# Attention followed by a softplus feed-forward network on one core: new places for attention's steps, the words of `at` and of the rests, and the accumulators' copies in the written queues of VectorE and ScalarE

## Chip, cores and metric

One core of a Trainium2 chip runs the whole kernel. The metric is the device time of one execution in microseconds (us); lower is better.

## What is computed

For each of 8 batches and 8 heads, 32 pack queries `p` attend over 576 keys and values, and then the 576 queries `q` attend over the 32 packed results, which serve as keys and as values. The heads, side by side, are the rows of `x` (4608 x 512), which goes through a feed-forward network with a softplus between its two products:

```python
p_packed = sm_attn(p, k, v)              # softmax(scale * p k^T) v
x = sm_attn(q, p_packed, p_packed)       # then heads side by side
h = x @ w_in                             # 512 -> 2048
g = np.maximum(h, 0.0) + np.log1p(np.exp(-np.abs(h)))
out = g @ w_out                          # 2048 -> 512
```

All is float32. The large products are made from float32r words: each factor is split into a high word and a low word (the rounding error of the high one), and three products of words are added.

## The kernel before

The main loop goes through **units** (b, f): 8 batches times 16 blocks of 128 columns of the hidden layer (L808). A unit has these parts.

- `gemm1` (L646): 12 matmuls of 288 columns into two PSUM banks of the pool `ps_h`, `ph` for columns 0 to 287 (c = 0) and 288 to 575 (c = 1). The moving data are `at_h` and `at_l`, the high and low words of the second attention's weights, which `weights` (L596) makes once per batch; the stationary data are `mh` and `ml`, the words of the pack results times `w_in` (`make_m`, L617, from a PSUM tile `psm`).
- `softplus` (L681): ScalarE takes `Abs`, `Exp` and `Ln` of each half (L691 to L693), VectorE adds the maximum (`e`, L699), which is the last read of a `ph` bank, and then `split` (L677) makes the words `gh` and `gl` of the result. GpSimd copies the last 64 rows to `rest` (L707).
- `gemm2_tile` (L713): two units later (`LAG`), 4 tiles t of 3 matmuls of 512 columns, which add into 4 accumulator banks `acc`. After the last f the four are copied to SBUF by `store` (L733) and sent out. The 64 left-over rows of two batches are added together in `rests` (L748) after every second batch: 48 matmuls into `acc_m`, from words `gh_m`, `gl_m`, which are made 256 columns at a time into two places.

Batches 2 to 7 get their attention from `attention_in_slots` (L495): `at(f, t, step)` puts a step into unit f of the batch before, after tile t of `gemm2_tile`; t = `END` (4) is behind all four. Names of steps: `move` transposes one 128x288 block of k or q on VectorE (`T_k`, `T_q`, L276); `score1` and `score2` are score matmuls into tiles `ps`; with `pair` (L506) they take the two `ps_h` banks. `score1`'s result is copied out by ScalarE, `score2`'s is transposed out by VectorE (L379). `max1` is a maximum over 576 columns (L319) and a scaling (L321); `exp2` and `div2` are the second softmax (L387, L388; L396 to L403).

From unit 16 on (L815) VectorE and ScalarE run their instructions in the order in which the program writes them, as TensorE does throughout. In a unit of batch 1 or later, `softplus` writes ScalarE's six functions at the start, `e` of half 0 behind the steps of t = 0, `e` of half 1 behind those of t = 2, and the split behind those of t = 3. The eight banks of PSUM are 4 for `acc`, 2 for `ps_h`, 2 for `psm` and the rest.

Of the kernel before, what the change touches and what calls it, by code (L numbers as in the profile page):

```python
# [26 lines left out]
def pack_attention_then_softplus_ffn(  # L27
# [10 lines left out]
    nc = tc.nc  # L38
# [3 lines left out]
    P = 128  # L42
# [452 lines left out]
    def attention_in_slots(b):  # L495
# [55 lines left out]

        END = NT
        early = b == BY_BLOCK
        for hh in range(HG):
            if early:
                at(hh // 2, hh % 2 * 2 + 1, move, "k", 0, hh)
                at(2, hh, move, "k", 1, hh)
            else:
                at(hh // 2 - 3, hh % 2 * (1 + (hh < 2)) + (hh < 2), move, "k", 0, hh)
                at(hh // 2 * 2, hh % 2 * (1 + (hh < 2)) + (hh < 2), move, "k", 1, hh)  # L560
            at(3 + hh // 2, 1 + hh % 2 * 2, move, "q", 0, hh)
            at(9 + hh // 2, hh % 2 * (1 + (hh < 2)) + (hh < 2), move, "q", 1, hh)
        if early:
            steps[(b - 1) * NF + 2, 0].insert(0, (score1, (0, False)))
            n = 2
        else:
            at(-2, END, score1, 0)
            n = 0
        at(-2 if not early else 2, END, load, "q", b, 0)
        at(n, 1 if early else 0, max1, 0)  # L570
        at(n, 2, exp1, 0)
        n = 3 if early else 2
        at(n, 0, sum1, 0)
        at(n, 0, turn1, 0, 0)
        at(n, 2, turn1, 0, 1)
        at(2, END, score1, 1)
        at(2, END, load, "q", b, 1)
        at(4, 0, max1, 1)
        at(4, 0, exp1, 1)
        at(5, 0, sum1, 1)  # L580
# [7 lines left out]
        for g in range(G):  # L588
            f = 6 + 4 * g
            at(f, END, score2, g)  # L590
            at(f, END, load, "v", b + 1, g)
            for c in range(2):
                at(f + 2, 2 * c, exp2, g, c)
                at(f + 3 + c, 2 * c, div2, g, c)

    def weights(b):  # L596

        at_h = work.tile([P, G, S], F32R, tag="at_h", name=f"at_h_{b}", bufs=1)
        at_l = work.tile([P, G, S], F32R, tag="at_l", name=f"at_l_{b}", bufs=1)
# [12 lines left out]

    def m_cols(b):
# [32 lines left out]
    def gemm1(b, f, res):  # L646

        n = m_cols(b)
        halves = res["m"][f * P // n]
        at_h, at_l = res["at"]  # L650
        phs = []
        for c in range(2):
            ph = ps_h.tile([P, 512], F32, tag="h", name=f"ph_{b}_{f}_{c}")
            phs.append(ph[:, :C])
            todo = [(g, j) for g in range(G) for j in range(3)]
            if f == 0 and b >= BY_BLOCK:
                todo.sort(key=lambda x: x[1] == 1)
            for i, (g, j) in enumerate(todo):
                mh, ml = halves[g * n // MC]
                o = g * n % MC + f * P % n  # L660
                cs = slice(c * C, (c + 1) * C)
                x, y = ((mh, at_h), (mh, at_l), (ml, at_h))[j]
                nc.tensor.matmul(  # L663
                    ph[:, :C], x[:, o:o + P], y[:, g, cs],
                    start=(i == 0), stop=(i == 3 * G - 1),
                )
                if (b, f, i) == (0, 0, 0) and c == 0:
                    busy(30, "at_l", (ps_acc, "acc"))
        return phs

    def halves(nm):
# [58 lines left out]
    def out_tile(nm):  # L730
        return cv.tile([P, 2, DM], F32, tag="x", name=f"o_{nm}", bufs=2)

    def store(o, acc, pieces, final=False):  # L733
        if final:
            n = DM // 2
            nc.vector.tensor_copy(o[:, :n], acc[:, :n])
            nc.scalar.copy(o[:, n:], acc[:, n:])
        else:
            nc.vector.tensor_copy(o, acc)  # L739
        for i, (row, b, col, n) in enumerate(pieces):  # L740
            queue = nc.scalar if final and i else nc.sync
            while n:
                to = rows_of(b, col)
                m = min(n, to.shape[0])
                queue.dma_start(to[:m], o[row:row + m, :])
                row, col, n = row + m, col + m, n - m

    def rests(b):  # L748


        fs = sorted(range(NF), key=lambda x: rest_at(b, x))
        gh, gl = halves(f"{b}_m")
        n = NT // 2
        for i in range(0, NF, n):
            o = rest_at(b, fs[i])
            c = i % NT * P
            cs = slice(c, c + n * P)
            split(gh[:, cs], gl[:, cs], rest[:, o:o + n, :].rearrange("x f j -> x (f j)"))
            if i == 0:
                yield  # L760
                am = ps_acc.tile([P, DM], F32, tag="acc", name=f"acc_{b}_m")
            for t in range(n):
                gemm2_tile(
                    am, gh, gl, fs[i + t], slice(c + t * P, c + (t + 1) * P),
                    i + t == 0, i + t == NF - 1,
                )
        pieces = [(0, b - 1, NT * P, REST), (REST, b, NT * P, REST)]
        store(out_tile(f"{b}_m")[:, 0], am, pieces, b == B - 1)
        yield


# [27 lines left out]
            next(conv)  # L799
            due -= 1  # L800
    make_m(0, 0, res[0])
    weights(0)
# [10 lines left out]
    for u in range(len(units) + LAG):  # L813
        if u == NF:
            ctx.enter_context(tc.manual_schedule(engines=ordered))  # L815
        if u < len(units):
# [24 lines left out]
        if last:  # L841
            both = rests(b2)
            next(both)
        for t in range(NT):
            if u >= LAG:
                gemm2_tile(
# [2 lines left out]
            if u < len(units):  # L849
# [56 lines left out]
```

## Time and profile before

| | us |
|---|---|
| median of 3 runs | 787.74 (786.58 to 788.06) |
| the profiled execution, its own time | 786.9 |
| its span | 785.1 |
| TensorE matmul busy | 745.4 (95% of the span) |
| VectorE busy | 552.9 (70%) |
| ScalarE busy | 464.7 (59%) |
| GpSimd busy | 91.6 (12%) |

The profiled execution's own time stands 1.8 us over its span and 0.8 us under the median. Busy time of TensorE is modelled from pipelined matmuls that overlap: a 288-column matmul is listed with 0.29 us, but the next starts 0.13 us later, so starts are to be compared, not durations. VectorE's and ScalarE's rows overlap a little as well.

### The profile page before, as it was taken

To read this page: it belongs to the slowest core of one execution; us is meant where nothing else is said; L and a number is where in the kernel's file an instruction comes from. 1 tells how busy PE (TensorE), PEld (TensorE's weight loads), DVE (VectorE), ACT (ScalarE), POOL (GpSimd) and SP (SyncE) were. 2 spreads that over 40 slices of the span, in tenths; PEclk is the share of its full clock that TensorE was granted. 3 is DMA by queue.
4 is the path that set the end of the run, shared out by engine and by line. 5 is a ranking of instruction groups with operands and counts; after the bars stand their busy time and mean duration, and the time that the engine had idled before them with its cause. 6 is when DMAs were issued, how large, how long until landed. Compare 5 with 4: busy or idle time off the path is not lost.

```text
span 785.1 us, 14466 instructions
## 1 busy us (share of the span) xinstructions
PE 745.4 (95%) x5436; PEld 595.5 (76%) x5436; DVE 552.9 (70%) x1264; ACT 464.7 (59%) x1086; POOL 91.6 (12%) x166
## 2 busy tenths in 40 slices
PE   6888998899999999999998999999999999999997
PEld 3766676678777887778886887788876787888886
DVE  2697899975877558776778568775778568775454
ACT  5668888565565455676555355666555355666650
POOL 1413443100000000000000000000000000000010
PEclk9878999999999999999999999999999999999999
DMA  9985756455222251125012251125113200010001
GB/s 213 239 186 150 180 157 153 81 108 99 40 33 57 44 91 31 31 78 97 10 26 70 58 92 30 28 72 92 18 31 71 58 2 1 1 54 1 1 1 68
DMA packets 163398, 55.98 MB, mean 71 GB/s; under 512 B 143872, under 2 KB 156672, under 8 KB 163328
## 3 DMA queue, kind: packets, MB, share of 16 engines
q1 hardware_dynamic: 162704, 54.80, 32.6%
q8 instruction: 42, 0.69, 0.4%
q10 hardware_dynamic: 624, 0.26, 0.1%
q14 instruction: 28, 0.23, 0.1%
HBM read 45.61 MB, written 9.44 MB: 70 GB/s over the span
## 4 chain that ended last, share of the span: by engine, by line
PE 66%; DVE 9%; ACT 4%; issue 1%; DVEq 0%; ACTq 0%
PE acc L715 33%; PE ph L663 21%; PE acc_m L715 5%; PE psm L625 3%; DVE e L699 2%; PE ps L294 1%; DVE at_l L607 1%; ACT e L692 1%; ACT e L693 1%; PE psa L339 1%; PE psp L353 1%; ACT e L691 1%; DVE gl L679 1%; DVE o L739 1%; DVE aT L403 1%
## 5 line engine op out<-in xcount | busy, mean ns | idle before, releaser
L691 ACT ACTIVATE e<-ph 128x288 f32<-128x288 f32 x256 | 103.0, 404 | 178.3 <-PE ph L663 161.1
L715 PE MATMUL acc<-wo_h,gh 128*128 128x512 f32 x512 | 204.2, 399 | 0.0
L715 PE MATMUL acc<-wo_l,gh 128*128 128x512 f32 x512 | 201.5, 394 | 0.0
L715 PE MATMUL acc<-wo_h,gl 128*128 128x512 f32 x512 | 201.3, 393 | 0.0
L699 DVE SCALAR_TENSOR_TENSOR e<-ph,e 128x288 f32<-128x288 f32 x256 | 114.5, 452 | 120.8 <-ACT e L693 120.8
L663 PE MATMUL ph<-at_h,mh 128*128 128x288 f32 x512 | 157.5, 308 | 8.9 <-DVE e L699 5.7
L663 PE MATMUL ph<-at_h,ml 128*128 128x288 f32 x512 | 151.3, 296 | 0.0
L663 PE MATMUL ph<-at_l,mh 128*128 128x288 f32 x512 | 149.9, 297 | 0.4 <-DVE at_l L607 0.2
L663 PEld LDWEIGHTS ph<-at_h,mh 128*128 128x128 f32 x512 | 96.8, 189 | 44.2 <-DVE a L379 11.4
L707 POOL COPY rest<-e 128x64 f32<-128x64 f32 x128 | 46.1, 361 | 590.6 <-DVE e L699 588.1
L692 ACT ACTIVATE e<-e 128x288 f32<-128x288 f32 (+1 forms) x240 | 110.6, 461 | 7.4
L693 ACT ACTIVATE e<-e 128x288 f32<-128x288 f32 (+1 forms) x240 | 110.6, 461 | 7.2
L715 PEld LDWEIGHTS acc<-wo_h,gl 128*128 128x128 f32 x512 | 96.5, 189 | 21.0
L715 PEld LDWEIGHTS acc<-wo_h,gh 128*128 128x128 f32 x512 | 96.5, 188 | 18.0 <-issue 2.3
L715 PEld LDWEIGHTS acc<-wo_l,gh 128*128 128x128 f32 x512 | 96.6, 189 | 14.8
L663 PEld LDWEIGHTS ph<-at_l,mh 128*128 128x128 f32 x512 | 96.4, 190 | 3.7 <-DVE at_l L607 1.0
L663 PEld LDWEIGHTS ph<-at_h,ml 128*128 128x128 f32 x512 | 96.8, 189 | 0.0
L679 DVE TENSOR_TENSOR gl<-e,gh 128x512 fp32r<-128x512 f32 x128 | 88.4, 691 | 8.3
L640 ACT CAST mh<-psm 128x512 fp32r<-128x512 f32 (+1 forms) x72 | 35.6, 541 | 46.6 <-PE psm L625 45.8
L678 DVE CAST gh<-e 128x512 fp32r<-128x512 f32 x128 | 55.8, 436 | 4.9
L641 DVE TENSOR_TENSOR ml<-psm,mh 128x512 fp32r<-128x512 f32 (+1 forms) x72 | 42.0, 621 | 19.7 <-ACT mh L640 19.7
L625 PE MATMUL psm<-w_in_sb,pt 64*32 64x512 f32 (+1 forms) x576 | 45.7, 561 | 2.4 <-DVE a L379 1.2
(79 smaller groups left out, 764.6 us busy)
## 6 DMA issues: line engine op xcount, KB each, us to landing
v<-in_v SPq DMA_DIRECT2D x16, 576.0 KB, 5.7
x_i<-in_moe_w_in SPq DMA_DIRECT2D x32, 256.0 KB, 4.5
x_o<-in_moe_w_out SPq DMA_DIRECT2D x16, 512.0 KB, 3.5
k<-in_k SPq DMA_DIRECT2D x48, 144.0 KB, 3.4
q<-in_q SPq DMA_DIRECT2D x48, 144.0 KB, 3.2
out<-o SPq DMA_DIRECT2D x24, 256.0 KB, 2.1
k<-in_k SPq DMA_DIRECT2D x4, 576.0 KB, 10.7
q<-in_q SPq DMA_DIRECT2D x4, 576.0 KB, 8.8
```

The lines of the kernel that those rows point to most:

```text
L625: nc.tensor.matmul(ps[hh * J:(hh + 1) * J, :n], res["pt"][g][o:o + D, hh * J:(hh + 1) * J], w_in_sb[o:o + D, hh, c * n:(c + 1) * n], start ...
L640: nc.scalar.copy(mh[:, cols], ps[:, :n])
L641: nc.vector.tensor_tensor(ml[:, cols], ps[:, :n], mh[:, cols].bitcast(F32), op=ALU.subtract)
L663: nc.tensor.matmul(ph[:, :C], x[:, o:o + P], y[:, g, cs], start=(i == 0), stop=(i == 3 * G - 1),)
L678: nc.vector.tensor_copy(hi, x)
L679: nc.vector.tensor_tensor(lo, x, hi.bitcast(F32), op=ALU.subtract)
L691: nc.scalar.activation(es[c], hv[c], AF.Abs)
L692: nc.scalar.activation(e[:, x], e[:, x], AF.Exp, scale=-1.0)
L693: nc.scalar.activation(e[:, x], e[:, x], AF.Ln, bias=1.0)
L699: nc.vector.scalar_tensor_tensor(es[c], hv[c], 0.0, es[c], op0=ALU.max, op1=ALU.add)
L707: nc.gpsimd.tensor_copy(rest[:, rest_at(b, f), r:r + REST], e[:, NT * P:])
L715: nc.tensor.matmul(acc, x[:, cs], y[:, f, :], start=(first and i == 0), stop=(last and i == 2),)
```

## The change

Four things move; nothing is computed differently.

1. Attention's steps get other places in the table: all `move` steps; `exp2` and `div2` of both halves go ahead of a unit's first `e`; `max1` of group 0 goes from ahead of unit 0's first `e` to behind it (in the steady batches), and in the first attention in slots (b = 2, `early`) the score and softmax steps of group 0 move by about a unit. In units with f = 10 (`late_split`) the split of `e` is written behind the steps of `END`.
2. `weights` becomes a generator: ScalarE casts `at_h` of group 0 only, VectorE casts group 1 (2 casts of 128x288 per batch), and `at_l` is made in two parts, on either side of unit 15's second `e`. In unit 0 of a batch, `gemm1` now runs all 8 products with `at_h` of both halves first and the 4 with `at_l` last, with the halves alternating.
3. `rests` makes two parts of its words before its first matmul, and each further part two groups of matmuls ahead.
4. The copies of accumulators 2 and 3 go from VectorE to ScalarE. The next pack of `p` is loaded in unit 1 and transposed in unit 6 (of batch 2), not 3 and 10.

```diff
+            moves = ((-4, 1), (-3, 1), (-2, 1), (-2, 3)), ((0, 1), (0, 2), (2, 0), (2, 1))
+        turns = ((2, END), (2, END), (3, 1), (4, 1)), ((8, 1), (9, 1), (10, 1), (10, 3))
...
-        at(n, 1 if early else 0, max1, 0)
-        at(n, 2, exp1, 0)
+        at(n, 1, max1, 0)
+        at(n, 1, exp1, 0)
...
-                at(f + 2, 2 * c, exp2, g, c)
-                at(f + 3 + c, 2 * c, div2, g, c)
+                at(f + 2, 0, exp2, g, c)
+                at(f + 3 + c, 0, div2, g, c)
...
+        for c in range(2):
+            high(nc.scalar.copy, 0, c)
+        yield
+        for c in range(2):
+            high(nc.vector.tensor_copy, 1, c)
+        for c in range(2):
+            low(0, c)
+        yield
+        for c in range(2):
+            low(1, c)
...
+        todo = [(c, g, j) for c in range(2) for g in range(G) for j in range(3)]
+        if f == 0 and b >= BY_BLOCK:
+            todo.sort(key=lambda x: (x[2] == 1, x[2] == 1 and x[1]))
...
+        for i in range(NT // n):
+            words(i)
+        yield
...
+            words(i + NT // n)
...
+    copies = nc.vector.tensor_copy, nc.scalar.copy
...
-                if f == 3:
+                if f == 1:
...
-                if f == 10:
+                if f == 6:
...
+        late_split = u < len(units) and b and f == 10
...
-            next(chain, None)
+            if not (late_split and t == NT - 1):
+                next(chain, None)
+            if t % 2 == 0:
+                next(words, None)
...
-                store(o[:, t % 2], acc[t], [(0, b2, t * P, P)])
+                store(o[:, t % 2], acc[t], [(0, b2, t * P, P)], copies[t // 2])
...
+            if late_split:
+                next(chain, None)
```

**Place 1: VectorE's queue in unit 10 of batch 4**, where attention of batch 5 makes its scores of group 1 (`ps_5_1_0`, `ps_5_1_1`). Before:

```order
L679 TENSOR_TENSOR gl_9_5767<-e_9_5733,gh_9_5766 128x512
L276 STREAM_TRANSPOSE T_q_1_2_5794<-q_1_5313 128x288
L699 SCALAR_TENSOR_TENSOR e_10_5784<-ph_10_0_5770,e_10_5784 128x288
L276 STREAM_TRANSPOSE T_q_1_3_5800<-q_1_5313 128x288
L396 TENSOR_REDUCE z_5_0_1_5805<-a_5_0_1_5609 128x9
L397 TENSOR_SCALAR z_5_0_1_5805<-z_5_0_1_5805 128x9
L398 RECIPROCAL z_5_0_1_5805<-z_5_0_1_5805 128x9
L399 TENSOR_TENSOR a_5_0_1_5609<-a_5_0_1_5609,z_5_0_1_5805 128x288
L403 STREAM_TRANSPOSE aT_0_1_5810<-a_5_0_1_5609 128x288
L699 SCALAR_TENSOR_TENSOR e_10_5784<-ph_10_1_5777,e_10_5784 128x288
L678 CAST gh_10_5817<-e_10_5784 128x512
```

The same place in the change:

```order
L403 STREAM_TRANSPOSE aT_0_1_5799<-a_5_0_1_5609 128x288
L716 SCALAR_TENSOR_TENSOR e_10_5784<-ph_10_0_5770,e_10_5784 128x288
L276 STREAM_TRANSPOSE T_q_1_2_5805<-q_1_5313 128x288
L716 SCALAR_TENSOR_TENSOR e_10_5784<-ph_10_1_5771,e_10_5784 128x288
L276 STREAM_TRANSPOSE T_q_1_3_5814<-q_1_5313 128x288
L379 STREAM_TRANSPOSE a_5_1_0_5822<-ps_5_1_0_5816 128x288
L379 STREAM_TRANSPOSE a_5_1_1_5828<-ps_5_1_1_5817 128x288
L695 CAST gh_10_5833<-e_10_5784 128x512
```

The five instructions of `div2` (from the reduction to `aT`) now stand ahead of both `e`, the fourth `T_q` stands behind the second `e`, and the two transposes that empty the score banks stand ahead of the split. Unit 14, with `T_k` and the next batch's `score1`, moves in the same way but keeps its split where it was.

**Place 2: VectorE's queue from unit 15 of batch 4 into unit 0 of batch 5** (`m_6_0` is `max1` of batch 6's attention). Before:

```order
L607 TENSOR_TENSOR at_l_6100<-aT_0_0_5748,at_h_6099 128x9x32
L607 TENSOR_TENSOR at_l_6100<-aT_0_1_5810,at_h_6099 128x9x32
L607 TENSOR_TENSOR at_l_6100<-aT_1_0_5972,at_h_6099 128x9x32
L607 TENSOR_TENSOR at_l_6100<-aT_1_1_6034,at_h_6099 128x9x32
L699 SCALAR_TENSOR_TENSOR e_15_6095<-ph_15_0_6081,e_15_6095 128x288
L699 SCALAR_TENSOR_TENSOR e_15_6095<-ph_15_1_6088,e_15_6095 128x288
```

The same place in the change:

```order
L716 SCALAR_TENSOR_TENSOR e_15_6095<-ph_15_0_6081,e_15_6095 128x288
L310 CAST at_h_6099<-aT_1_0_5974 128x9x32
L310 CAST at_h_6099<-aT_1_1_6023 128x9x32
L608 TENSOR_TENSOR at_l_6100<-aT_0_0_5750,at_h_6099 128x9x32
L608 TENSOR_TENSOR at_l_6100<-aT_0_1_5799,at_h_6099 128x9x32
L716 SCALAR_TENSOR_TENSOR e_15_6095<-ph_15_1_6082,e_15_6095 128x288
L608 TENSOR_TENSOR at_l_6100<-aT_1_0_5974,at_h_6099 128x9x32
L608 TENSOR_TENSOR at_l_6100<-aT_1_1_6023,at_h_6099 128x9x32
```

The first `e` no longer stands behind the four `at_l`, and two casts have come to VectorE.

**Place 3: VectorE's queue in unit 0 of batch 5.** Before:

```order
L319 TENSOR_REDUCE m_6_0_6155<-a_6_0_6045 128x1
L321 TENSOR_SCALAR nm_6_0_6157<-m_6_0_6155 128x1
L699 SCALAR_TENSOR_TENSOR e_0_6145<-ph_0_0_6131,e_0_6145 128x288
L276 STREAM_TRANSPOSE T_k_1_0_6163<-k_1_5522 128x288
L699 SCALAR_TENSOR_TENSOR e_0_6145<-ph_0_1_6138,e_0_6145 128x288
L276 STREAM_TRANSPOSE T_k_1_1_6174<-k_1_5522 128x288
```

The same place in the change:

```order
L716 SCALAR_TENSOR_TENSOR e_0_6145<-ph_0_0_6131,e_0_6145 128x288
L276 STREAM_TRANSPOSE T_k_1_0_6159<-k_1_5522 128x288
L319 TENSOR_REDUCE m_6_0_6161<-a_6_0_6045 128x1
L321 TENSOR_SCALAR nm_6_0_6163<-m_6_0_6161 128x1
L276 STREAM_TRANSPOSE T_k_1_1_6170<-k_1_5522 128x288
L716 SCALAR_TENSOR_TENSOR e_0_6145<-ph_0_1_6132,e_0_6145 128x288
```

Two transposes and the maximum now stand between the first and the second `e`.

## Rows read from the trace of the kernel before

In the timelines the columns are start, duration (both us), engine, line, operation, tiles out<-in, shapes, count, and in brackets the engine's idle time just before and what ended it.

**Rows 1.** The first part of the page, all engines: busy us (share of the span) and instructions.
```profile
PE 745.4 (95%) x5436; PEld 595.5 (76%) x5436; DVE 552.9 (70%) x1264; ACT 464.7 (59%) x1086; POOL 91.6 (12%) x166
```

**Rows 2.** The waits of TensorE from 150 us to the end: waiting line, releaser, total us, times, longest.
```profile
PE ps L294 <- DVE e L699: 5.8, 11, 1.5
PE acc_m L715 <- DVE gh_m L678: 3.8, 3, 1.3
PE ph L663 <- DVE e L699: 2.0, 6, 0.4
```

**Rows 3.** Timeline of TensorE at the end of unit 10 of batch 4: the two halves of `score2`, and the first `ph` matmul of unit 11 (`psm` in between).
```profile
486.83 0.69 PE L294 MATMUL ps<-T_q,pt 64*32 64x288 f32 x8
487.96 0.45 PE L294 MATMUL ps<-T_q,pt 64*32 64x288 f32 x4 [0.44 <-DVE e L699]
...
489.68 0.40 PE L663 MATMUL ph<-at_h,mh 128*128 128x288 f32 x1 [0.17 <-DVE a L379]
```

**Rows 4.** Timeline of VectorE in the same unit: first `e`, `T_q`, the start of `div2`, second `e`.
```profile
484.92 0.46 DVE L699 SCALAR_TENSOR_TENSOR e<-ph,e 128x288 f32<-128x288 f32 x1 [0.80 <-ACT e L693]
485.29 0.47 DVE L276 STREAM_TRANSPOSE T_q<-q 128x288 f32<-128x288 f32 x1
485.69 0.41 DVE L396 TENSOR_REDUCE z<-a 128x9 f32<-128x288 f32 x1
...
487.49 0.42 DVE L699 SCALAR_TENSOR_TENSOR e<-ph,e 128x288 f32<-128x288 f32 x1
```

**Rows 5.** Timeline of TensorE at the end of unit 2 of batch 5: the same kind of score block, and the `ph` behind it.
```profile
528.59 0.71 PE L294 MATMUL ps<-T_k,pT 64*32 64x288 f32 x16
...
530.09 0.40 PE L663 MATMUL ph<-at_h,mh 128*128 128x288 f32 x1
```

**Rows 6.** The same at the end of unit 14 of batch 4.
```profile
507.21 0.69 PE L294 MATMUL ps<-T_k,pT 64*32 64x288 f32 x8
...
509.81 0.40 PE L663 MATMUL ph<-at_h,mh 128*128 128x288 f32 x1
```

**Rows 7.** The same at the end of unit 10 of batch 2, the unit that begins with the transposes of the next pack.
```profile
308.08 0.88 PE L294 MATMUL ps<-T_q,pt 64*32 64x288 f32 x8
...
312.01 0.40 PE L663 MATMUL ph<-at_h,mh 128*128 128x288 f32 x1
```

**Rows 8.** The same at the end of unit 2 of batch 1, in the first attention in slots.
```profile
169.48 1.55 PE L294 MATMUL ps<-T_k,pT 64*32 64x288 f32 x11
...
172.06 0.40 PE L663 MATMUL ph<-at_h,mh 128*128 128x288 f32 x1
```

**Rows 9.** Timeline of ScalarE from unit 15 of batch 4 on: the casts of `at_h`, `Abs` and `Ln` of unit 15's second half, and `Abs` of the first half of unit 1.
```profile
512.23 1.42 ACT L310 CAST at_h<-aT 128x288 fp32r<-128x288 f32 x4
513.55 0.40 ACT L691 ACTIVATE e<-ph 128x288 f32<-128x288 f32 x1
...
514.46 0.44 ACT L693 ACTIVATE e<-e 128x288 f32<-128x288 f32 x1
...
520.21 0.41 ACT L691 ACTIVATE e<-ph 128x288 f32<-128x288 f32 x1 [0.96 <-PE ph L663]
```

**Rows 10.** Timeline of VectorE in the same stretch: `at_l`, the first `e` of unit 15; `max1`, the first `e` and a `T_k` of unit 0; the first `e` of unit 1.
```profile
512.67 1.57 DVE L607 TENSOR_TENSOR at_l<-aT,at_h 128x288 fp32r<-128x288 f32 x4 [1.27 <-ACT at_h L310]
514.15 0.45 DVE L699 SCALAR_TENSOR_TENSOR e<-ph,e 128x288 f32<-128x288 f32 x1
...
516.50 0.75 DVE L319 TENSOR_REDUCE m<-a 128x1 f32<-128x576 f32 x1
...
517.36 0.46 DVE L699 SCALAR_TENSOR_TENSOR e<-ph,e 128x288 f32<-128x288 f32 x1
517.73 0.47 DVE L276 STREAM_TRANSPOSE T_k<-k 128x288 f32<-128x288 f32 x1
...
521.67 0.46 DVE L699 SCALAR_TENSOR_TENSOR e<-ph,e 128x288 f32<-128x288 f32 x1 [1.21 <-ACT e L693]
```

**Rows 11.** Timeline of TensorE in the same stretch: the last `acc` matmul of unit 15, the first `ph` of unit 0, the first and the seventh `ph` of unit 1.
```profile
514.05 0.39 PE L715 MATMUL acc<-wo_h,gl 128*128 128x512 f32 x1
514.75 0.37 PE L663 MATMUL ph<-at_h,mh 128*128 128x288 f32 x1 [0.32 <-DVE e L699]
...
519.16 0.29 PE L663 MATMUL ph<-at_h,mh 128*128 128x288 f32 x1
...
519.95 0.29 PE L663 MATMUL ph<-at_h,mh 128*128 128x288 f32 x1
```

**Rows 12.** Timeline of TensorE in unit 1 of batch 4: the sixth and the seventh matmul of `acc_m`.
```profile
429.57 0.39 PE L715 MATMUL acc_m<-wo_h,gl_m 128*128 128x512 f32 x1
431.23 0.50 PE L715 MATMUL acc_m<-wo_h,gh_m 128*128 128x512 f32 x1 [1.27 <-DVE gh_m L678]
```

**Rows 13.** Timeline of VectorE there: the copy of accumulator 3, and the second part's high word.
```profile
430.29 0.68 DVE L739 COPY o<-acc 128x512 f32<-128x512 f32 x1
430.89 0.28 DVE L678 CAST gh_m<-rest 128x256 fp32r<-128x256 f32 x1
```

**Rows 14.** Timeline of VectorE in unit 8 of batch 4: first `e`, the maximum of `exp2`'s second half, second `e`.
```profile
476.26 0.46 DVE L699 SCALAR_TENSOR_TENSOR e<-ph,e 128x288 f32<-128x288 f32 x1 [0.67 <-ACT e L693]
476.64 0.44 DVE L387 TENSOR_REDUCE m<-a 128x9 f32<-128x288 f32 x1
...
477.49 0.45 DVE L699 SCALAR_TENSOR_TENSOR e<-ph,e 128x288 f32<-128x288 f32 x1
```

More of the change, by code (lines that the diff above doesn't have):

```diff
@@ L553, in attention_in_slots @@
         early = b == BY_BLOCK
[L554 to L562, printed above, removed]
-        if early:
-            steps[(b - 1) * NF + 2, 0].insert(0, (score1, (0, False)))
-            n = 2
+        if early:
+            moves = ((0, 1), (0, 2), (0, 3), (1, 0)), ((2, 0), (2, 0), (2, 1), (2, 3))
+        else:
+            moves = ((-4, 1), (-3, 1), (-2, 1), (-2, 3)), ((0, 1), (0, 2), (2, 0), (2, 1))
+        turns = ((2, END), (2, END), (3, 1), (4, 1)), ((8, 1), (9, 1), (10, 1), (10, 3))
+        for what, places in (("k", moves), ("q", turns)):
+            for g in range(G):
+                for hh, place in enumerate(places[g]):
+                    if (what, g, hh) == ("q", 0, 0):
+                        at(2, END, score1, 1)
+                        at(2, END, load, "q", b, 1)
+                    at(*place, move, what, g, hh)
+        if early:
+            at(1, 3, score1, 0, False)
+            at(1, 3, load, "q", b, 0)
+            n = 3
         else:
             at(-2, END, score1, 0)
+            at(-2, END, load, "q", b, 0)
             n = 0
-        at(-2 if not early else 2, END, load, "q", b, 0)
-        at(n, 1 if early else 0, max1, 0)
-        at(n, 2, exp1, 0)
-        n = 3 if early else 2
+        at(n, 1, max1, 0)
+        at(n, 1, exp1, 0)
+        n = 4 if early else 2
         at(n, 0, sum1, 0)
@@ L650, in gemm1 @@
         at_h, at_l = res["at"]
[L651 to L668, printed above, removed]
+        phs = [
+            ps_h.tile([P, 512], F32, tag="h", name=f"ph_{b}_{f}_{c}")[:, :C] for c in range(2)
+        ]
+        todo = [(c, g, j) for c in range(2) for g in range(G) for j in range(3)]
+        if f == 0 and b >= BY_BLOCK:
+            todo.sort(key=lambda x: (x[2] == 1, x[2] == 1 and x[1]))
+        for i, (c, g, j) in enumerate(todo):
+            mh, ml = halves[g * n // MC]
+            o = g * n % MC + f * P % n
+            cs = slice(c * C, (c + 1) * C)
+            x, y = ((mh, at_h), (mh, at_l), (ml, at_h))[j]
+            mine = [k for k, y in enumerate(todo) if y[0] == c]
+            nc.tensor.matmul(
+                phs[c], x[:, o:o + P], y[:, g, cs], start=(i == mine[0]), stop=(i == mine[-1]),
+            )
+            if (b, f, i) == (0, 0, 0):
+                busy(30, "at_l", (ps_acc, "acc"))
         return phs
@@ L738, in store @@
         else:
[L739 removed]
+            copy(o, acc)
         for i, (row, b, col, n) in enumerate(pieces):
@@ L753, in rests, with words @@
         n = NT // 2
[L754 to L761, printed above, removed]
+        parts = [slice(i % NT * P, (i % NT + n) * P) for i in range(0, NF, n)]
+        def words(i):
+            if i < len(parts):
+                o = rest_at(b, fs[i * n])
+                x = rest[:, o:o + n, :].rearrange("x f j -> x (f j)")
+                split(gh[:, parts[i]], gl[:, parts[i]], x)
+        for i in range(NT // n):
+            words(i)
+        yield
+        am = ps_acc.tile([P, DM], F32, tag="acc", name=f"acc_{b}_m")
+        for i, cs in enumerate(parts):
             for t in range(n):
[L763 to L766, printed above, removed]
+                c, f = cs.start + t * P, i * n + t
+                gemm2_tile(am, gh, gl, fs[f], slice(c, c + P), f == 0, f == NF - 1)
+            words(i + NT // n)
         pieces = [(0, b - 1, NT * P, REST), (REST, b, NT * P, REST)]
-        store(out_tile(f"{b}_m")[:, 0], am, pieces, b == B - 1)
+        store(out_tile(f"{b}_m")[:, 0], am, pieces, final=b == B - 1)
         yield
@@ L801, in pack_attention_then_softplus_ffn @@
     make_m(0, 0, res[0])
-    weights(0)
+    for _ in weights(0):
+        pass
     busy(12, "at")
@@ L827, in pack_attention_then_softplus_ffn @@
             next(chain)
+            words = iter(())
             if f == NF - 1:
```

26 lines of the change are left out of this document (14 added, 12 removed).

## The prediction

> **What bounds the kernel now.** I read the page's first part, then TensorE's waits, then the timelines of the places where TensorE stands still. The page gives TensorE 95% of the span and VectorE 70% [rows 1]; the matmuls are the same before and after, so only TensorE's standing time can be won. After 150 us, where VectorE and ScalarE follow written queues, it waits in few places, and nearly always for VectorE: 11 times in a score block, 3 times in the rests, 6 times at the first unit of a batch [rows 2]. Those rows show only the part of a wait that no pipelined matmul covers, so I price a wait by the distance between starts. From the first score matmul of an undisturbed block to the next `ph` are 1.50 us [rows 5]. The block of unit 10 takes 2.85 [rows 3], that of unit 14 2.60 [rows 6], unit 10 of batch 2 3.93 [rows 7], the first attention's block in unit 2 2.58 [rows 8]: 1.35, 1.10, 2.43 and 1.08 too much. Why is plain in VectorE's rows: the second half of the scores needs the bank that the second `e` empties, and that `e` stands behind a transpose and the five instructions of `div2`, so it starts at 487.49, while the first `e` was at 484.92 [rows 4].
>
> **A. Score blocks.** Unit 10 stands five times with 1.35 and once with 2.43, unit 14 five times with 1.10, the early block once with 1.08: 6.75 + 2.43 + 5.50 + 1.08 = 15.76 us. With `div2` ahead, the second `e` waits only for ScalarE, whose three functions of a half take 1.35 (513.55 to 514.90) [rows 9]; it then comes at about 486.2, 1.3 earlier. What is late next is the fourth `T_q` (or `T_k`), now behind that `e`: 486.2 + 0.37 + 0.47 = 487.05, and 0.15 until TensorE sees it (as from 514.60 to 514.75 in [rows 10, 11]), 487.2 against the block's start at 486.83 [rows 3]. Three of the four heads can run meanwhile; the residue lies between 0 and 0.4, and I take 0.15 for each of 12 blocks, 1.8. Behind the block, the transposes of the score banks stand ahead of the split, and 1.1 us of `psm` matmuls lie between: no wait for them. The pack's transposes, now in unit 6 of batch 2, do there what they did in unit 10: 3.93 - 2.85 = 1.08 [rows 3, 7], through pT copies that hold up ScalarE. They also follow at once on `turn_pack`, whose banks they need: between 0 and two copies of 0.28 [rows 13], I take 0.4. So A gives 15.76 - 1.8 - 1.5 = **12.5**.
>
> The Trainium skill, Perfetto Trace Analysis, section "Optimization Strategy", speaks against this: the same gap repeating on the engine that should be full can mean that there isn't enough PSUM for the next tile. The banks stay as they are here; by that rule A would be 0 and the whole sum 3.2. Against it stands that the same kind of block with the same banks runs undisturbed in unit 2 [rows 5].
>
> **B. Start of a batch.** A `ph` matmul starts 0.13 after the one before it (0.79 for six), an `acc` matmul 0.24 (a twelfth of what 12 of the former leave of the 4.41 between 514.75 and 519.16) [rows 11]. So unit 0 could start at 514.05 + 0.24 = 514.29; it does at 514.75: 0.46, six times. It waits for the first `e`, which stood behind four `at_l` (1.57), which stood behind ScalarE's casts (1.42) [rows 9, 10]. Now the first `e` comes first, and ScalarE has two casts less, 0.66 off the second half. VectorE gets two casts of 288 columns, 0.28 (256 columns, [rows 13]) to 0.39 each (a quarter of 1.57); the second `e` could start at 514.90 - 0.66 = 514.24, or 0.2 later if VectorE is behind, and its bank is free 0.61 later (below: 0.46 + 0.15), at 514.85 to 515.05. The fifth matmul wants it at 514.29 + 4 x 0.13 = 514.81. Residue 0 to 0.24, taken 0.07: 6 x 0.39 = **2.3**.
>
> **C. Rests.** From the sixth to the seventh matmul are 1.66 instead of 0.24 [rows 12], since the second part's words stand behind the accumulators' copies on VectorE (430.29, 430.89) [rows 13]. Now they are ready before the first matmul, and later parts are two groups ahead: 1.42 three times, 4.3. Price: one part more ahead of unit 1's first `e`, so accumulator 0's bank, which `acc_m` takes, may come up to 0.1 late: **4.0** remains. The copies that go to ScalarE fall between unit 1's and unit 2's functions, where it waits for TensorE (0.96 idle before 520.21, [rows 9]): nothing. So do `exp2` and `T_q` at (2, END): the first `e` of unit 8 had 0.67 of idle time [rows 14] and the added pair takes 0.85 (476.64 to 477.49); the 0.2 left over is inside the second half's own time.
>
> **D. A new wait.** Let S be unit 0's start. The first half now ends with the eleventh matmul instead of the sixth: 5 x 0.13 = 0.66 later. `Abs` came 1.05 after a unit's start and `e` 1.46 behind that [rows 9 to 11]; here `e` starts at S + 1.05 + 0.66 + 1.46 = S + 3.17. Then come 0.37 for itself, 0.40 for a `T_k` [rows 4], 0.86 for the maximum and its scaling [rows 10], 0.40 for the other `T_k`: the second `e` starts at S + 5.20 and with 0.46 + 0.15 its bank is free at S + 5.81. TensorE wants it at unit 1's seventh matmul, S + 4.41 + 0.79 = S + 5.20 [rows 11]. It loses 0.61 at each of the five batch starts that have a `max1` (batches 2 to 6): **-3.1**. Before, the maximum lay ahead of the first `e`, in the time that ScalarE needed.
>
> The Trainium skill, Perfetto Trace Analysis, section "Matmuls", wants independent groups to take turns over banks so that one is evacuated while the next computes. The alternating halves of unit 0 give that up; by the rule alone the 0.66 would be lost at all six starts, 4.0 instead of 3.1, and the sum 0.9 smaller.
>
> **Sum.** 12.5 + 2.3 + 4.0 - 3.1 = 15.7 us off the profiled execution's 786.9, which is 0.8 under the median: 787.74 - 15.7 = **772.0** (2.0% less).
>
> **Rivals.**
> 1. D stays away, because VectorE gets through the five instructions in the time that ScalarE needs. Against it stand the durations above. 787.74 - 15.7 - 3.1 = 768.9. Chance 0.14.
> 2. The late fourth transpose costs more than I took, 0.5 at each of 12 blocks (just over the upper bound), 4.2 more, and B's residue its 0.24 (1.0 more): 777.2. Chance 0.16.
> 3. The banks are the limit, A's gain is nil: 787.74 - 3.2 = 784.5. Chance 0.05.
> 4. Slower. Work put ahead of a unit's first `e` makes VectorE the bound in units 8 and 12, as in D: both `exp2` pairs, 1.7, now stand there, and `T_q` or `T_k` between the halves; if each second `e` comes so late that TensorE waits at the next unit's seventh matmul, 12 places pay. They outweigh the gain from 15.7/12 = 1.3 each on, and at 1.5 the time is 787.74 - 15.7 + 18 = 790.0. Against it: with the 0.67 of idle time [rows 14] only 0.2 is added ahead of the first `e`. Chance 0.05.
> 5. The gains are taken up by waits for ScalarE that now come to light, and nothing is left: 787.7. For it speaks little, since ScalarE is busy 59% [rows 1]. Chance 0.03.
>
> **How the numbers follow.** My forecast has 0.57. Its own range is 769.5 to 776, from the bounds of the residues: 12 x 0.15, B's 0.4 and the pack's 0.4 less, or 12 x 0.25 and B's 1.0 more. The range of 8 in 10 reaches to rivals 1 and 2: 767 to 779; outside are rivals 3 to 5 with 0.13. A measurement of this kernel can tell about 0.2% (1.6 us) from no change. Faster by more are the forecast and rivals 1 to 3, 0.92; no change is rival 5, 0.03; slower is rival 4, 0.05.
>
> **What would show it.** Right: score blocks of units 10 and 14 of 1.5 to 1.8 us instead of 2.85 and 2.60; unit 0's first `ph` within 0.1 of the last `acc`; no gap between the sixth and the seventh matmul of `acc_m`; a new wait of about 0.7 at the seventh `ph` of unit 1 for `e`, in batches 2 to 6 but not in 7; a longer start of unit 6 and a late block in batch 2. Wrong: blocks that still take over 2 us, waits for `e` in units 9 and 13, or no wait in unit 1.

## The result, and the profile after

The change takes 769.2 us (767.87 to 772.59, five runs) instead of 787.74: a ratio of 0.9773 with a 95% interval of 0.9748 to 0.9797, 18.5 us less. The forecast was 772.0. The profiled execution of the change took 767.87 us, its span 766.1.

The first part of its page, as in [rows 1]:

```profile
PE 734.3 (96%) x5436; PEld 594.0 (78%) x5436; DVE 550.9 (72%) x1260; ACT 469.1 (61%) x1090; POOL 94.0 (12%) x166
```

TensorE has as many matmuls as before, and 19 us of span are gone. TensorE's waits from 150 us on, as in [rows 2], columns as there:

```profile
PE ph L681 <- DVE e L716: 1.7, 5, 0.4
PE ppt L109 <- DVE pt L370: 0.3, 1, 0.3
```

The 11 waits in score blocks, the 3 in the rests and the 6 at the start of a batch are no longer listed; 5 waits of a new kind are, and one short one for the pack. (Before had one kind more, which [rows 2] leave out: five waits of `ph` for the transposes `a` of L379, 0.9 us in all, such as the 0.17 in [rows 3]. They stood inside the blocks that are priced by starts, and are gone too.)

**A score block.** TensorE at the end of unit 10 of batch 4 (the place of [rows 3]; all score matmuls stand in one row, since the second half follows at once):

```profile
474.74 0.87 PE L294 MATMUL ps<-T_q,pt 64*32 64x288 f32 x16
475.25 1.22 PE L643 MATMUL psm<-w_in_sb,pt 64*32 64x512 f32 x16
476.39 0.40 PE L681 MATMUL ph<-at_h,mh 128*128 128x288 f32 x1
```

VectorE in the same unit (the place of [rows 4]): the end of `div2`, both `e`, the third and the fourth `T_q`, the first split.

```profile
472.83 0.48 DVE L403 STREAM_TRANSPOSE aT<-a 128x288 f32<-128x288 f32 x1
473.23 0.42 DVE L716 SCALAR_TENSOR_TENSOR e<-ph,e 128x288 f32<-128x288 f32 x1
473.57 0.46 DVE L276 STREAM_TRANSPOSE T_q<-q 128x288 f32<-128x288 f32 x1
474.01 0.46 DVE L716 SCALAR_TENSOR_TENSOR e<-ph,e 128x288 f32<-128x288 f32 x1
474.38 0.47 DVE L276 STREAM_TRANSPOSE T_q<-q 128x288 f32<-128x288 f32 x1
```

The block takes 476.39 - 474.74 = 1.65 instead of 2.85. The second `e` begins 0.73 ahead of the block; before, it began 0.66 behind the block's start (487.49 against 486.83). The fourth `T_q` ends 0.11 behind the block's start, and that it is late costs 0.15 against the undisturbed 1.50 [rows 5].

**The start of a batch.** TensorE from the last `acc` of unit 15 of batch 4 to the seventh `ph` of unit 1 (as [rows 11]):

```profile
499.79 0.39 PE L732 MATMUL acc<-wo_h,gl 128*128 128x512 f32 x1
500.01 0.29 PE L681 MATMUL ph<-at_h,mh 128*128 128x288 f32 x1
...
505.12 0.29 PE L681 MATMUL ph<-at_h,ml 128*128 128x288 f32 x1
505.75 0.40 PE L681 MATMUL ph<-at_h,mh 128*128 128x288 f32 x1 [0.34 <-DVE e L716]
```

Unit 0 starts 0.22 behind the last `acc`, without a wait (before 0.70). The new wait is at the seventh `ph` of unit 1: 0.63 after the sixth instead of 0.13, so 0.50. VectorE in unit 0 shows why (the place of [rows 10]):

```profile
503.31 0.46 DVE L716 SCALAR_TENSOR_TENSOR e<-ph,e 128x288 f32<-128x288 f32 x1 [0.98 <-ACT e L710]
503.68 0.47 DVE L276 STREAM_TRANSPOSE T_k<-k 128x288 f32<-128x288 f32 x1
504.07 0.71 DVE L319 TENSOR_REDUCE m<-a 128x1 f32<-128x576 f32 x1
504.82 0.15 DVE L321 TENSOR_SCALAR nm<-m 128x1 f32<-128x1 f32 x1
504.89 0.47 DVE L276 STREAM_TRANSPOSE T_k<-k 128x288 f32<-128x288 f32 x1
505.28 0.42 DVE L716 SCALAR_TENSOR_TENSOR e<-ph,e 128x288 f32<-128x288 f32 x1
```

VectorE stands idle for 0.98 and then has five instructions in a row; the last of them is the one that TensorE waits for. With S = 500.01, the first `e` is at S + 3.30 (forecast S + 3.17) and the second at S + 5.27 (S + 5.20).

**The rests.** TensorE in unit 1 of batch 4, the first, the sixth and the seventh matmul of `acc_m` (as [rows 12]):

```profile
417.72 0.50 PE L732 MATMUL acc_m<-wo_h,gh_m 128*128 128x512 f32 x1
...
418.98 0.39 PE L732 MATMUL acc_m<-wo_h,gl_m 128*128 128x512 f32 x1
419.21 0.39 PE L732 MATMUL acc_m<-wo_h,gh_m 128*128 128x512 f32 x1
```

The seventh follows 0.23 after the sixth; 1.66 it was. (The first comes 0.32 after the last `acc`, at 417.40, where 0.23 is the rule: the 0.1 that the forecast set aside for a late accumulator bank. The second comes 0.34 after the first, 0.1 more.)

**The next pack,** now in unit 6 of batch 2. TensorE, with the block at the unit's end, and then ScalarE:

```profile
276.78 1.06 PE L109 MATMUL ppt<-ident,p 128*64 128x128 f32 x8 [0.27 <-DVE pt L370]
277.60 0.38 PE L681 MATMUL ph<-at_h,mh 128*128 128x288 f32 x1
...
282.13 1.28 PE L294 MATMUL ps<-T_q,pt 64*32 64x288 f32 x12
...
284.55 0.40 PE L681 MATMUL ph<-at_h,mh 128*128 128x288 f32 x1
```

```profile
278.61 1.18 ACT L112 COPY pT<-ppt 64x512 f32<-64x512 f32 x2 [4.87 <-DVE pT L111]
279.81 0.41 ACT L708 ACTIVATE e<-ph 128x288 f32<-128x288 f32 x1
```

ScalarE's pT copies wait for VectorE's, so unit 6's functions begin only at 279.81, 2.21 after its first `ph`, and the block at its end takes 2.42. Both the longer start and the late block were forecast.

### The profile page after: what moved, and what is told of

The parts are those of the page before. It is cut to its first block, busy times and chain, and to the rows that moved or that the text cites. A ratio compares the mean times of both kernels' runs of the same rounds, so it can differ in the third digit from the quotient of the medians.

```text
span 766.1 us, 14465 instructions
## 1 busy us (share of the span) xinstructions
PE 734.3 (96%) x5436; PEld 594.0 (78%) x5436; DVE 550.9 (72%) x1260; ACT 469.1 (61%) x1090; POOL 94.0 (12%) x166
## 4 chain that ended last, share of the span: by engine, by line
PE 76%; DVE 2%; ACT 1%; issue 0%; DVEq 0%; ACTq 0%
PE acc L732 39%; PE ph L681 23%; PE acc_m L732 6%; PE psm L643 3%; PE ps L294 2%; PE psp L353 1%; PE psa L339 1%; DVE T_k L276 1%; DVE m L319 0%; ACT e L709 0%; ACT e L710 0%; DVE e L716 0%; ACT e L708 0%; PE psx L368 0%; DVE nm L321 0%
## 5 line engine op out<-in xcount | busy, mean ns | idle before, releaser
L724 POOL COPY rest<-e 128x64 f32<-128x64 f32 x128 | 48.6, 380 | 570.4 <-DVE e L716 568.2
L643 PE MATMUL psm<-w_in_sb,pt 64*32 64x512 f32 (+1 forms) x576 | 41.5, 546 | 3.6 <-DVE a L379 2.1
```

The lines of the kernel that those rows point to most:

```text
L643: nc.tensor.matmul(ps[hh * J:(hh + 1) * J, :n], res["pt"][g][o:o + D, hh * J:(hh + 1) * J], w_in_sb[o:o + D, hh, c * n:(c + 1) * n], start ...
L724: nc.gpsimd.tensor_copy(rest[:, rest_at(b, f), r:r + REST], e[:, NT * P:])
```

## Where the time went, by units

I take the distance between the first `ph` of each unit and the next in both traces. From unit 16 (where the written queues begin) to the end, before takes 630.07 us and the change 614.03: 16.04 less.

| term | forecast | measured, sum over the units |
|---|---|---|
| A, blocks without the pack (15.76 - 1.8) | 14.0 | unit 10: 1.24, 2.37, 1.17, 3 x 1.19 = 8.35; unit 14: 4.45; early block, units 1 to 4 of batch 1: 0.99; together 13.8 |
| A, the pack in unit 6 | -1.5 | unit 5 +1.33, unit 6 +0.93, unit 9 -0.79: -1.5 |
| B, six batch starts | 2.3 | 0.49 to 0.51 each, 3.0 |
| C and D, unit 1 | 4.0 - 3.1 = 0.9 | batches 2 to 6: -0.76, +0.62, -0.72, +0.60, -0.66: 0.9 |
| sum | 15.7 | 16.2, and 0.2 lost in other units |

Batches 3 and 5 have no rests, so D stands there alone: 0.62 and 0.60. In batches 2, 4 and 6 it stands beside C, and only their sum can be read here. In batch 7 there is no wait, as forecast. At the seventh `ph` the distance to the sixth is 0.62 to 0.65 in batches 2 to 6 and 0.13 in batch 7.

The medians differ by 18.5, 2.5 more than this. In the two profiled executions, 19.0 apart, what goes beyond the 16.0 lies ahead of unit 16: before reaches it at 155.03, the change at 152.07, and up to there both have the same instructions in the same order. The first two experiments are about that.

## The experiments

"Rest" is the time from unit 16 to the end of the span, the part that the change reorders, read from the one profiled execution of each kernel (spans are listed to 0.1 us). Each kernel is the change with one thing undone, unless said otherwise. Each ratio is against executions of before that were made beside the kernel; their medians are 787.74 (the change), 785.56 (before_again to old_weights), 785.80 (max_first) and 786.03 (best).

| run | median us (runs) | ratio to before, 95% | unit 16 at | rest |
|---|---|---|---|---|
| before, shown above | 787.74 | | 155.03 | 630.07 |
| the change, shown above | 769.2 (5) | 0.9773 (0.9748 to 0.9797) | 152.07 | 614.03 |
| before_again | 785.33 (12) | 0.9994 (0.9971 to 1.0017) | 152.21 | 631.69 |
| after_again | 770.0 (4) | 0.9799 (0.9772 to 0.9826) | 154.69 | 613.91 |
| old_table | 778.86 (4) | 0.9917 (0.9888 to 0.9946) | 155.64 | 623.36 |
| old_weights | 768.84 (4) | 0.9785 (0.9757 to 0.9814) | 154.36 | 613.04 |
| old_rests | 770.99 (1) | | 153.65 | 615.55 |
| old_copies | 772.25 (1) | | 153.40 | 616.50 |
| old_rests_old_copies | 773.41 (1) | | 153.09 | 618.51 |
| split_in_place | 767.57 (1) | | 151.60 | 614.20 |
| max_first | 766.06 (4) | 0.9748 (0.9728 to 0.9769) | 153.12 | 610.28 |
| max_first_old_weights | 768.24 (1) | | 151.61 | 613.49 |
| best | 762.58 (5) | 0.9701 (0.9678 to 0.9725) | 152.85 | 608.25 |

The rest is the sharper measure: that of the change came out within 0.12 in two executions, while unit 16 was at 151.60 to 155.64 over these 13. That of before differed by 1.62, nearly all of it in one unit (below), so I compare kernels unit by unit as well. Five kernels were executed once; what is said of them rests on that one trace.

**before_again and after_again: both kernels once more, without an edit.**

> The kernel before, once more, for the stretch ahead of the change. Up to the start of unit 16 both kernels hold the same instructions in the same order on every engine, yet that start came at 155.0 us in the trace of before and at 152.1 after, and the medians are 18.5 us apart where the stretches from unit 16 on are 16.0 apart. Theory 1: the start varies from run to run and the change has no part in it; unit 16 will start anywhere from 151 to 156 us, and the stretch from there to the end is 630.1 +- 0.5. Rival: something of the changed program (placement, code) speeds the start; unit 16 starts again at 154.5 or later.

> The changed kernel, once more. Theory 1: the stretch from the start of unit 16 to the end is 614.0 +- 0.5 us, and unit 16 starts anywhere from 151 to 156. Rival: unit 16 starts again at 152.5 or earlier. The time stays 2.0 to 2.5% under before under both.

The second time the gain is 785.56 - 770.0 = 15.6 us, and it is now the change whose unit 16 comes late. So the extra 2.5 us of the first comparison need not be the change's, and the rival (the changed program speeds the start) fell: unit 16 came at 152.21 in before and at 154.69 in the change. What goes with it, roughly, is the clock that TensorE was granted there: the six traces whose unit 16 comes at 153.40 or later have 0.83 to 0.86 from 40 to 80 us, the seven earlier ones 0.87 to 0.96. The stretch from 40 to 80 us of the change in its two executions (span of the stretch, then busy time of PE, PEld, DVE, ACT and POOL, the granted clock, DMA share, GB/s), first the one with unit 16 at 152.07, then the one at 154.69:

```profile
40.00:80.00 40.00, 32.57 (x256) 24.26 (x253) 33.86 (x80) 30.44 (x69) 12.72 (x13) 0.96 0.69 174
```

```profile
40.00:80.00 40.00, 33.99 (x245) 25.03 (x246) 32.32 (x77) 28.91 (x64) 11.41 (x12) 0.85 0.70 169
```

Before stands at 0.83 in this stretch. What sets the clock there was not tried.

The rest of before_again is 1.62 longer than that of before, outside the 0.5 that was expected; 1.50 of it is unit 11 of batch 2. In the late block just ahead of it, in unit 10 [rows 7], TensorE stood for 1.47 us in both, and this time the clock fell behind it (the end of the wait, then two stretches of before_again, columns as above):

```profile
307.70 0.45 PE L294 MATMUL ps<-T_q,pt 64*32 64x288 f32 x4 [1.47 <-DVE e L699]
...
309.60:313.00 3.40, 3.40 (x15) 3.28 (x15) 1.52 (x3) 2.05 (x5) 0.00 (x0) 0.55 0.00 0
313.00:316.40 3.40, 3.40 (x20) 3.00 (x19) 2.44 (x6) 1.00 (x3) 0.49 (x1) 1.00 0.02 5
```

At 0.55 it is nearly all at the lower level, 1.2 GHz; `ph` matmuls start 0.24 apart there and 0.13 apart from 315.25 on, at 2.4 GHz. Before had the same wait of 1.47 and kept 1.00 (309 to 315.4 us). The change's block there takes 1.65.

**old_table: the places of attention's steps as before** (the table and the split; the pack, the words and the copies stay new).

```diff
+            at(3 + hh // 2, 1 + hh % 2 * 2, move, "q", 0, hh)
+            at(9 + hh // 2, hh % 2 * (1 + (hh < 2)) + (hh < 2), move, "q", 1, hh)
...
-        turns = ((2, END), (2, END), (3, 1), (4, 1)), ((8, 1), (9, 1), (10, 1), (10, 3))
...
-        at(n, 1, max1, 0)
...
+        at(n, 1 if early else 0, max1, 0)
...
-                at(f + 2, 0, exp2, g, c)
-                at(f + 3 + c, 0, div2, g, c)
+                at(f + 2, 2 * c, exp2, g, c)
+                at(f + 3 + c, 2 * c, div2, g, c)
...
-        late_split = u < len(units) and b and f == 10
+        late_split = False
```

> The changed kernel with the table of places of before (moves, exp2, div2, max1, first attention) and the split of unit 10 in its old place; the pack's transposes stay in unit 6, and weights, rests and copies stay new. Theory 1 (terms of the prediction): the score blocks are back at 2.9 and 2.6 us, which costs 12 us, and the wait in unit 1 goes, since the maximum is back ahead of the first e, which gives 3: the stretch from unit 16 on is 614 + 9 = 623 us. Rival (banks set the blocks, the table does little): 616 or less.

TensorE at the end of unit 10 of batch 4:

```profile
483.58 0.69 PE L294 MATMUL ps<-T_q,pt 64*32 64x288 f32 x8
484.71 0.45 PE L294 MATMUL ps<-T_q,pt 64*32 64x288 f32 x4 [0.44 <-DVE e L714]
...
486.43 0.40 PE L679 MATMUL ph<-at_h,mh 128*128 128x288 f32 x1 [0.17 <-DVE a L379]
```

The block is back at 2.85, 11 such waits are back, and the new wait in unit 1 is gone with the old place of `max1`. The rest is 9.4 longer than the change's: 13.8 of blocks come back, less the 3.0 of D and the 1.08 that the pack no longer adds to unit 10 of batch 2, makes 9.7. Most of the change's gain is the table. The table was put back whole; that it is `div2` in units 10 and 14, and not another step, is read from the queue (one transpose stands between the two `e` before and after; `div2` alone leaves), not tried alone.

**split_in_place: only the late split of unit 10 undone.**

```diff
-        late_split = u < len(units) and b and f == 10
+        late_split = False
```

> The changed kernel without the late split: unit 10's split stands ahead of the score transposes. Theory 1: the transposes come 1.1 us later, which the 1.1 us of psm matmuls behind the scores nearly cover, so the first ph of unit 11 waits 0.1 to 0.3 us, five or six times: 614 + 1 us from unit 16 on. Rival (the late split is what frees the score banks in time): blocks of 2.4 us or more, 614 + 4 or more.

Rest 614.20 against 614.03 and 613.91, and no unit from batch 2 on differs (one of batch 1 by 0.26). The late split is worth nothing. The expectation of 615 was 0.8 too high, since the transposes do not come 1.1 later: VectorE in unit 10 of batch 4, the score transposes in the change and then here.

```profile
475.61 0.85 DVE L379 STREAM_TRANSPOSE a<-ps 128x288 f32<-128x288 f32 x2 [0.76 <-PE ps L294]
```

```profile
475.60 0.84 DVE L379 STREAM_TRANSPOSE a<-ps 128x288 f32<-128x288 f32 x2
```

In the change VectorE stands idle for 0.76 until the scores are there. Here the split fills that time, and the transposes start 1.14 behind the block's start (474.46) instead of 0.87 (474.74), which the matmuls of `psm` cover.

**old_weights: `weights` and the order of unit 0's matmuls as before.**

```diff
-        for c in range(2):
-            high(nc.scalar.copy, 0, c)
...
+        for g, c in parts:
+            high(nc.scalar.copy, g, c)
+            low(g, c)
+        return
...
-            todo.sort(key=lambda x: (x[2] == 1, x[2] == 1 and x[1]))
+            todo.sort(key=lambda x: (x[0], x[2] == 1))
```

> The changed kernel with weights all at once (all four casts on ScalarE) and with unit 0's products half by half as before. Theory 1: the wait at unit 0's first matmul is back (0.5 at each of six batch starts, 2.9 us lost), but the first half ends 0.66 earlier again, so that the second e of unit 0 has its bank free at about the time that it is wanted and the 0.6 us wait in unit 1 goes at five starts (3.0 won): together 614 +- 0.7, no difference. Rival: the wait in unit 1 comes from the maximum alone, whatever the order of the products, and stays: 617.

TensorE's waits from 150 us on in old_weights:

```profile
PE ph L673 <- DVE e L708: 2.0, 6, 0.3
PE ppt L109 <- DVE pt L370: 0.3, 1, 0.3
PE ps L294 <- DVE e L708: 0.2, 1, 0.2
```

The six waits at the starts of batches return (0.49 a unit), and all five waits in unit 1 vanish, although `max1` still stands behind the first `e`: with one half after the other, the first half ends with the sixth matmul, and VectorE's first `e` comes at S + 2.58 instead of S + 3.30. Undoing this part makes the rest 0.9 shorter, a little outside the 0.7 that was expected: by units, D gives 3.3 back and B costs 3.0; 0.28 more is a block in batch 3 (last section), and what remains is spread. So in this change the part lost slightly more through D than it won by B. The medians, 768.84 and 769.2 or 770.0, do not tell the two apart.

**max_first: only `max1` goes back ahead of unit 0's first `e`.**

```diff
-        at(n, 1, max1, 0)
+        at(n, 1 if early else 0, max1, 0)
```

> The changed kernel with one step moved: max1 of group 0 ahead of unit 0's first e, as before, in batches 2 to 6; all else new. Theory 1: VectorE has that time free (its queue ends at unit 0's start + 2.2 us, the first e starts at + 3.3), so the first e is not late, the second comes 0.7 earlier, and the wait at unit 1's seventh matmul (0.5 shown, 0.6 by starts, five times) goes: 614 - 3 = 611 us from unit 16 on, about 766 in all. Rival: the maximum makes the first e late by as much, and nothing is won.

VectorE in unit 0 of batch 5, from the maximum to the second `e`:

```profile
501.05 0.74 DVE L319 TENSOR_REDUCE m<-a 128x1 f32<-128x576 f32 x1
501.83 0.15 DVE L321 TENSOR_SCALAR nm<-m 128x1 f32<-128x1 f32 x1
502.12 0.46 DVE L716 SCALAR_TENSOR_TENSOR e<-ph,e 128x288 f32<-128x288 f32 x1
502.49 0.83 DVE L276 STREAM_TRANSPOSE T_k<-k 128x288 f32<-128x288 f32 x2
503.30 0.46 DVE L716 SCALAR_TENSOR_TENSOR e<-ph,e 128x288 f32<-128x288 f32 x1
```

and TensorE's sixth and seventh `ph` of unit 1:

```profile
503.91 0.29 PE L681 MATMUL ph<-at_h,ml 128*128 128x288 f32 x1
504.04 0.29 PE L681 MATMUL ph<-at_h,mh 128*128 128x288 f32 x1
```

The maximum runs in the time in which VectorE stood idle, the second `e` comes 1.18 after the first instead of 1.97, and the seventh `ph` follows the sixth after 0.13. Unit 1 is shorter by 0.73, 0.61, 0.75, 0.60 and 0.80 in batches 2 to 6, the rest by 3.7, more than the 3 expected. Moving this one step takes D away. The batches with rests gain 0.1 to 0.2 more than the others: there the first `acc_m` now comes 0.23 after the last `acc`, not 0.32, and the second 0.23 after it. So the late accumulator bank, too, hung on the late maximum, and not only on the part of words that the prediction charged it to (in old_rests, without that part, it is gone as well).

**max_first_old_weights: both of the last two.**

> The kernel with the maximum first, with weights all at once on ScalarE and unit 0's products half by half as before. With the late maximum this undoing won 1.0 us. Theory 1: the two parts work on the same slack; without the late maximum there is no wait in unit 1 to be won back, so only the wait at unit 0's start returns, 0.49 at six batch starts: 610.3 + 2.9 = 613.2 us from unit 16 on. Rival (the order of the products is a loss of its own): 610 or less.

613.49, 3.2 over max_first. Of this 3.0 is the wait at six batch starts; a wait of 0.5 for `e`, which the other kernels do not have, makes unit 4 of batch 1 longer by 0.9, and other units give some back, so the part is worth 2.4 to 3.2 here. The second part of the change, a small loss beside the late `max1` (0.9 in the rest, 0.3 by D and B alone), is a gain beside the early one: what it is worth is set by the place of another instruction.

**old_rests, old_copies, and both.** The words of the rests as before, and the copies of all four accumulators on VectorE:

```diff
-        for i in range(NT // n):
-            words(i)
+        words(0)
...
+            if i:
+                words(i)
...
-            words(i + NT // n)
```

```diff
-    copies = nc.vector.tensor_copy, nc.scalar.copy
+    copies = nc.vector.tensor_copy, nc.vector.tensor_copy
```

> The changed kernel with the rests' words one part at a time, as before; the copies of accumulators 2 and 3 stay on ScalarE. Theory 1 (the prediction put the whole 1.4 per place on the words being late behind the accumulators' copies on VectorE; with two of these gone the words come about 1.2 us earlier by themselves): between the sixth and seventh matmul of acc_m stand 0.3 to 0.6 us of waiting instead of 1.4, and from unit 16 on it takes 614 + 1.5 us. Rival (the words' own place is all): 1.4 at three places, 618.

> The changed kernel with all four accumulators' copies on VectorE, as before; the rests' words stay two parts ahead. Theory 1: VectorE gets 1.2 us more in unit 1, the third part of the rests' words comes late instead of the second, and acc_m waits about 1 us at its thirteenth matmul, three times: 614 + 3 us from unit 16 on. Rival (the words two parts ahead cover everything, the copies' engine is of no matter): 614.

> The changed kernel with the rests' words one part at a time and all accumulators' copies on VectorE, both as before. Alone they cost 1.5 and 2.5 us from unit 16 on. Theory 1: they queue on the same engine in the same unit, so together they cost the whole 1.4 of before at each of three places, less what the wait in unit 1 covers: 614 + 4 us. Rival (either alone already costs what both cost): 616.5.

TensorE at the first late `acc_m` matmul of batch 4, with the one before it: in old_rests (the seventh),

```profile
420.95 0.39 PE L732 MATMUL acc_m<-wo_h,gl_m 128*128 128x512 f32 x1
421.78 0.50 PE L732 MATMUL acc_m<-wo_h,gh_m 128*128 128x512 f32 x1 [0.44 <-DVE gh_m L695]
```

in old_copies (later, since two parts are ready),

```profile
422.31 0.39 PE L732 MATMUL acc_m<-wo_h,gl_m 128*128 128x512 f32 x1
423.13 0.50 PE L732 MATMUL acc_m<-wo_h,gh_m 128*128 128x512 f32 x1 [0.44 <-DVE gh_m L695]
```

and in both.

```profile
421.14 0.39 PE L732 MATMUL acc_m<-wo_h,gl_m 128*128 128x512 f32 x1
422.93 0.50 PE L732 MATMUL acc_m<-wo_h,gh_m 128*128 128x512 f32 x1 [1.41 <-DVE gh_m L695]
```

Starts are 0.83, 0.82 and 1.79 apart instead of 0.23. The rest grows by 1.6, 2.5 and 4.5: either measure alone brings the delay of 1.56 down to 0.6, and the rest of it takes both. In the old_copies kernels unit 1 of batch 5 is longer by 0.4 as well, where there are no rests: its wait at the seventh `ph` is 0.69 instead of 0.34, since the first `e` of unit 0 ran only after ScalarE's `Abs` of the second half. Why was not followed.

**best: max_first, and two more moves.** The last transpose goes one tile earlier, so that it stands ahead of the second `e` again, now that `div2` is out of the way; the pack goes from unit 6, which ends in a score block, to unit 12, which does not.

```diff
...
-            moves = ((-4, 1), (-3, 1), (-2, 1), (-2, 3)), ((0, 1), (0, 2), (2, 0), (2, 1))
-        turns = ((2, END), (2, END), (3, 1), (4, 1)), ((8, 1), (9, 1), (10, 1), (10, 3))
+            moves = ((-4, 1), (-3, 1), (-2, 1), (-2, 2)), ((0, 1), (0, 2), (2, 0), (2, 1))
+        turns = ((2, END), (2, END), (3, 1), (4, 1)), ((8, 1), (9, 1), (10, 1), (10, 2))
...
-                if f == 6:
+                if f == 12:
```

> The changed kernel with max1 of group 0 ahead of unit 0's first e (batches 2 to 6), the fourth T_q of unit 10, the fourth T_k of unit 14 and of the first attention ahead of the second e instead of behind it (t = 2 for t = 3), and the next pack's transposes in unit 12 of batch 2 instead of unit 6. Theory 1: from the 610.3 us that the moved maximum alone gives from unit 16 on, the fourth transpose takes 0.15 at each of about 11 score blocks away (1.6), and unit 12, which has no score block, loses 0.8 for the pack's matmuls and at most 0.6 for ScalarE's late copies, where units 5 and 6 lost 2.3: 608 us, about 763.5 in all. Rival: the transpose ahead of the second e makes that e late by as much as it gains; 609.5 or more.

TensorE in the block of unit 10 of batch 4:

```profile
471.78 0.73 PE L294 MATMUL ps<-T_q,pt 64*32 64x288 f32 x16
...
473.31 0.40 PE L681 MATMUL ph<-at_h,mh 128*128 128x288 f32 x1
```

1.53: the residue of 0.15 is nearly gone (0.12 to 0.14 a block in batches 3 to 6, 0.07 to 0.08 in batches 1 and 2), units 5 and 6 of batch 2 are 2.26 shorter, and units 11 and 14 take 1.2 of that back. 762.58 us is 0.9701 of before (0.9678 to 0.9725), and from 150 us on the trace lists no wait of TensorE (gaps of up to 0.15 us are not listed).

## Why the prediction was right

**A** was right in mechanism and size: 12.3 against 12.5. The banks come free with the second `e`, and that came late only through the queue ahead of it; the table alone, put back, brings the 2.85 us block back. The residue of 0.15 was taken from a range of 0 to 0.4 without a sum for it, so that it came out exactly in 10 of the 12 blocks is partly luck; the two others kept 0.44 (unit 14 of batch 3) and 0.27 (the early block). That the residue is the fourth transpose is shown by best. The Trainium skill, Perfetto Trace Analysis, section "Optimization Strategy", takes repeating gaps on the engine that should be full as a possible sign of too little PSUM. Here there were enough: with the same banks the block fell from 2.85 to 1.65, and to 1.53 in best (rival 3).

**B** was right in mechanism and 3.0 instead of 2.3 in size: the term's residue of 0.07 a start does not exist, and the last `acc` took 0.22 instead of the 0.24 that I set aside. Undoing it brings back 0.49 a start.

**C** came out at 4.0 if D is given 0.6 in every batch, as in the two without rests. By max_first D costs 0.7 to 0.8 beside the rests; then C is 4.4 and D 3.5 instead of 3.1. Only their sum, 0.9, does not depend on where the late accumulator bank is charged. The words ahead and the copies on ScalarE each carry part of it, which the prediction had not priced apart: 1.6 and 2.5 in the rest when undone alone, 4.5 together.

**D** was right: five waits, 0.5 at the matmul and 0.6 in the unit, in the batches that have a `max1`. Its two causes were shown apart: put `max1` first, or let the first half end with the sixth matmul, and the wait is gone. The Trainium skill, Perfetto Trace Analysis, section "Matmuls", wants independent groups to rotate over banks, so that one is emptied while the next computes; by the rule alone all six starts would pay. Five paid, and none in max_first, where the halves still alternate: here giving up the overlap cost only where the engine that empties the bank had no spare time. So rival 1 fell, and rivals 2 and 4 with it (residues of 0.15, and no waits in units 9 and 13).

**The sum** was 15.7, and the reordered part lost 16.0; B's 0.7 more, A's 0.2 less and 0.2 lost in other units make the difference. The medians' 18.5 goes beyond that, in the profiled executions by the start of 150 us, which the change does not touch; repeated, it was 15.6. So the median of 769.2 lies 2.8 under the forecast of 772.0, just outside the forecast's own range (769.5 to 776; its terms as listed add up to 769.4 at the lower end), and nearest to rival 1 (768.9), whose mechanism the traces refute. A reader of the medians alone would have picked the wrong account.

## What to carry to other kernels

Read a repeated wait of the main engine for a buffer back to the queue of the engine that empties it: what stands ahead of the emptying instruction, and could it stand in that engine's own idle time? Price such a wait, and what takes its place, by the distance between starts, and write down for each moved instruction which one it now precedes. When a change has several parts, try them apart and together: one that lost 0.3 to 0.9 us here gained 2.4 or more as soon as a two-instruction maximum went back to where VectorE was idle.

## What was not expected

- The first 150 us vary by 4 us between executions of the same order (151.60 to 155.64), and TensorE's granted clock from 40 to 80 us, 0.83 to 0.96, goes with it roughly; what causes either was not found. That is a quarter of the gain that was to be measured; the distance from a fixed place in the program was the better measure.
- After one and the same 1.47 us wait the clock stayed at 1.00 in one execution and stood at 0.55 from 309.6 to 313.0 us in another, which made unit 11 of batch 2 1.5 us longer. A wait of TensorE can cost more than its length.
- One block of unit 14 in batch 3 kept 0.3 us more than the others in the change (a second `e` that waited 0.26 for ScalarE) and lost it in old_weights, best and three other kernels. It was not followed further.
